# Splitting each weight once instead of once per batch, and one pool of seven buffers for it

## The chip, the core and the metric

The kernel runs on one core of a Trainium2 chip. The metric is device time in microseconds. The kernel before was timed three times: 928.41 us is the median, 927.8 the lowest and 928.49 the highest. The profile comes from one further execution, whose own span, from its first to its last instruction, is 930.6 us.

The core has these engines: PE (TensorE, the matrix multiplier; PEld is its loading of the stationary operand), DVE (VectorE), ACT (ScalarE), POOL (GpSimd) and SP (SyncE). Here SP only issues DMAs, in the order of its queue: a DMA whose buffer is not yet free holds up the DMAs behind it.

## The reference

Softcapped attention for 4 batches, 12 heads, 448 tokens and a head size of 64, then a gated feed-forward block over all 4 x 448 tokens.

```python
scores = cap * np.tanh(scale * (q @ k^T) / cap)
attn = exp(scores - max) / (sum(...) + 1e-09)
x = (attn @ v), heads side by side      # 1792 x 768
gate = 1 / (1 + np.exp(-(x @ w_gate)))  # w_gate, w_val: 768 x 1536
out = (gate * (x @ w_val)) @ w_out      # w_out: 1536 x 768
```

The activations come as float32. The weights reach the kernel as float64.

## The kernel before

**The arithmetic.** TensorE multiplies float32 values as pairs: x = hi + lo, where hi is x rounded to a shorter format (float32r) and lo = x - hi. A product is hi*lo + hi*hi + lo*hi, three passes. So every operand has to be *split*: `o.hi` (line 148; "p" is POOL, line 151) writes the rounded part, and `o.lo` (line 157; "v" is DVE, line 159) writes the rest. All splits by these helpers stand in the profile under lines 151 and 159, and are told apart by the tile they write.

**The weights.** The three weight matrices are cut into 36 units of 128 x 768 values: per group of four columns blocks of w_gate, four units, then four of w_val (24 units in all), then 12 units of w_out. The feed-forward of a batch uses units 0 to 35 in this order, and each of the four batches does so again: 144 uses, numbered u = 0 to 143.

- `load_w64` (line 590) loads a unit as float64, 768 KB, into one of three buffers (`w`).
- `convert_w` (line 596) makes float32 of it from the bits: one ACT instruction (line 609) and three DVE instructions (lines 610 to 612), into one of four buffers (`wx`, tag `wraw`). The float32 unit is then stored to DRAM (`wd`, 384 KB).
- `load_w` (line 635) reads a float32 unit back from DRAM into one of the same four buffers (`wraw`). That is needed for the first 12 units, which are converted during batch 0's attention and not kept (`o.early`), and for all units of batches 1 to 3: 120 loads of 384 KB.
- `split_w` (line 641) splits a unit with POOL and DVE into one of three buffers (`wspl`), two units ahead of its use. It runs for all 144 uses.
- `next_w` (line 674) is called before a unit's matmuls. It converts up to four units ahead during batch 0, loads three ahead, and splits two ahead.

**The stages.** Batch 0's attention runs alone (with the conversion of the first 12 units beside it). Then the feed-forward of batch b runs beside the attention of batch b+1, and the feed-forward of batch 3 runs alone at the end. The feed-forward has two parts: `h` (line 690, 24 units of 18 matmuls with 448 columns) and `o` (line 761, 12 units; 18 matmuls of 384 columns each, 30 in the last batch, which also takes the left-over tokens of all batches).

**Attention of batches 1 to 3.** Per head: transposes (line 282), scores (line 307), tanh and exp on ACT (lines 310 and 442), the split of the exponentials (`ph` on ACT at line 153, `pl` and the last part of `ph` on DVE), the sum over keys in three POOL additions (`a`, lines 317 to 319), in batches 2 and 3 a fold on DVE (line 322), the split of the sum (`as`: POOL, then DVE), the matmul of the sums (`dn`, line 395) and the product with V (`pv`, lines 381 to 384).

**What sets the order.** A list scheduler orders the instructions of each engine at build time. It takes the program order and its own estimate of when buffers come free. During batch 0's attention the order of PE and ACT is the one in which the code is written. On the chip each engine then works through its own list in order: where an instruction waits, everything behind it on that engine waits too.

Of the kernel before, what the change touches and what calls it, by code (L numbers as in the profile page):

```python
# [23 lines left out]
# Up to here exp(score) needs no maximum: |score| <= |cap|, so that every exponential lies between  # L24
# exp(-32) and exp(32).
# [4 lines left out]
def tile_softcap_attention_then_gated_ffn(  # L30
# [11 lines left out]
    """Softcapped attention, then a gated feed-forward block, in float32.  # L42

    TensorE multiplies float32 operands as pairs of float32r values: x = hi + lo, where hi is x
    rounded to 12 significant bits and lo = x - hi is exact, so hi*hi + hi*lo + lo*hi carries the
    product to float32's accuracy at one pass each.

    The softmax has two forms, chosen by the value of cap: exponentials of the scores as they are
    where cap bounds them, and with the maximum subtracted for any other cap.
    """  # L50
# [9 lines left out]
    # The first pair of heads is on its way before cap chooses.  # L60
# [8 lines left out]
    # TensorE's clock rises with some microseconds of work.  # L69
# [4 lines left out]
    # The score is even in cap.  # L74
# [20 lines left out]
def _load(nc, t, src, n, twice):  # L95
    """Both heads of pair n; the chunk after the full ones holds the last tokens, on either half
    when twice."""
# [15 lines left out]
def _load_heads_inside(nc, t, src, n):  # L113
    """The same, with both heads of a token side by side, and the last tokens once."""
# [12 lines left out]
class _Ops:  # L127
    """What both attentions share."""

    def __init__(self, tc, ctx, c, q, k, v):  # L130
# [4 lines left out]
        self.FULL = self.S // P * P  # tokens in the chunks of 128  # L135
# [12 lines left out]
    def hi(self, eng, dst, src):  # L148
        """dst (float32r) = src rounded."""
        if eng == "p":  # L150
            self.nc.gpsimd.tensor_scalar(dst, src, 1.0, 1.0, ALU.mult, ALU.mult)  # L151
        elif eng == "a":
            self.nc.scalar.activation(dst, src, AF.Copy)  # L153
        else:
            self.nc.vector.tensor_copy(dst, src)
# [12 lines left out]
def _bounded_attention(o, x_done):  # L168
    """Scores with keys on partitions; yields the PE passes (of 448 columns) that it has emitted,
    and None after a batch.  # L170

    Of the reference's denominator, sum(exp(s - max)) + 1e-9, both terms are taken times exp(max):
    sum(exp(s)) + 1e-9 * exp(max). The sum stands in for exp(max), which it bounds: in float32 the
    guard leaves a sum that holds exp(max) as it is.
    """
# [5 lines left out]
    # The sums of GS heads stand on one row each, rows 0.. (repeated up to 32): head i's stationary  # L181
    # operand has ones in the columns of its rows. Their reciprocals, hi on rows 0.., lo on rows
    # 32.., go to the 64 rows of each head through spread.
# [17 lines left out]
    # The first batch has TensorE to itself: products of its first heads are plain float32.  # L201
# [8 lines left out]
    def spare(h):  # L210
        """VectorE converts weights during the first two batches."""
# [23 lines left out]
    def split_pair(n):  # L235
# [6 lines left out]
        if n < NP and direct_v(2 * n):  # L242
            # Beside each head's V a block of ones, for the sums.
# [17 lines left out]
    def emit_T(h, step=None):  # L261
        """k and q with tokens along the free dimension: both heads of a pair in float32, or
        [hi; lo] of one head and q's [lo; hi]."""
# [71 lines left out]
    def emit_P(h):  # L335
        """The exponentials, split. The last chunk's upper copy becomes its low part."""
# [10 lines left out]
    def emit_PV(h):  # L347
# [6 lines left out]
        if direct_v(h):  # L354
            # The sums stand on the partitions of the other head.
# [30 lines left out]
        # The rows of V_hi and of V_lo meet on the partitions that the head has in x.  # L386
# [72 lines left out]
def _general_attention(o, x_done):  # L459
    """Queries on partitions, with each row's maximum subtracted; products are plain float32."""  # L460
# [87 lines left out]
def _emit(tc, ctx, c, attention_of, q, k, v, w_gate, w_val, w_out, out):  # L548
# [10 lines left out]
    WRAW = 4  # L559
    AHEAD = 2  # L560
# [296 lines left out]
```

## Time and profile before

| | |
|---|---|
| time, median of 3 (lowest to highest) | 928.41 us (927.8 to 928.49) |
| span of the profiled execution | 930.6 us |
| PE busy | 825.7 us, 89% |
| DVE busy | 709.5 us, 76% |
| POOL busy | 526.4 us, 57% |
| ACT busy | 458.2 us, 49% |
| DMA | 119.77 MB, 129 GB/s over the span |

Rows of instruction groups read: line, engine, operation, tile written <- tiles read, shapes, number; then busy time in us and the mean of one in ns; then the idle time of the engine just before these instructions and what ended most of it. In a table by stretches of time each row gives the stretch, its length, and for each engine the busy time and the number of instructions in it, then the granted TensorE clock as a share of full speed, the mean busy share of the 16 DMA engines, and GB/s. Rows of waits read: who waited <- for whom: us in total, times, longest. Busy time on PE includes slower running at a lower granted clock.

### The profile page before, as it was taken

The page shows a single profiled execution, that of the slowest core. Times are in us where ns is not written, and L with a number is a line of the kernel's source. Part 1 is how long each engine was busy: PE and PEld are TensorE (multiplying, and loading weights), DVE is VectorE, ACT ScalarE, POOL GpSimd, SP SyncE. Part 2 cuts the span into 40 slices and gives each one's busy share as a digit, 9 for nine tenths or more (in the row PEclk, how much of TensorE's full clock was granted, in tenths as well). Part 3 has the DMA queues.
Part 4 walks back from the last instruction along what each step waited for, and adds up shares of the span by engine and source line. Part 5 has one row for each costly group of instructions (what it writes and reads, how often), then busy time and mean ns, then how long its engine had stood idle before and what let it go on. Part 6 is the DMA issues. An engine that isn't in the chain of part 4 may idle for free. (4 is left out here: it accounts for less than half of the span.)

```text
span 930.6 us, 10942 instructions
## 1 busy us (share of the span) xinstructions
PE 825.7 (89%) x3890; PEld 696.3 (75%) x3890; DVE 709.5 (76%) x664; ACT 458.2 (49%) x601; POOL 526.4 (57%) x468
## 2 busy tenths in 40 slices
PE   8998899787886768988998798999898999999994
PEld 4443487666775757877887687888787889999994
DVE  0586877999999999798968898799959985455220
ACT  4796685573375642846446661848365612101000
POOL 1233689668588875675739565677738643233110
PEclk6998999888997889999999999999999999999998
DMA  6497842363557445323332534223232464334211
GB/s 171 134 281 237 260 133 76 122 213 108 166 172 218 153 134 158 91 63 103 86 118 59 140 109 135 91 80 102 74 119 63 122 191 134 111 122 120 73 61 46
DMA packets 114408, 119.77 MB, mean 129 GB/s; under 512 B 53928, under 2 KB 91304, under 8 KB 114344
## 3 DMA queue, kind: packets, MB, share of 16 engines
q1 hardware_dynamic: 114344, 118.98, 42.1%
q8 instruction: 33, 0.54, 0.2%
q14 instruction: 31, 0.25, 0.1%
HBM read 96.14 MB, written 22.02 MB: 127 GB/s over the span
## 5 line engine op out<-in xcount | busy, mean ns | idle before, releaser
L690 PE MATMUL h<-xspl,wspl 128*128 128x448 f32 x1728 | 397.5, 376 | 16.4 <-DVE wspl L159 12.6
L690 PEld LDWEIGHTS h<-xspl,wspl 128*128 128x128 f32 x1728 | 330.2, 193 | 53.4 <-DVE wspl L159 15.9
L159 DVE TENSOR_TENSOR wspl<-wraw,wspl 128x768 fp32r<-128x768 f32 x120 | 153.3, 1284 | 92.5 <-POOL wspl L151 90.6
L151 POOL TENSOR_SCALAR wspl<-wraw 128x768 fp32r<-128x768 f32 x120 | 116.9, 977 | 152.4 <-PE h L690 62.2
L761 PE MATMUL o<-wspl,gspl 128*128 128x384 f32 x864 | 175.2, 353 | 19.0 <-DVE wspl L159 17.4
L761 PEld LDWEIGHTS o<-wspl,gspl 128*128 128x128 f32 x864 | 161.9, 200 | 24.5 <-DVE wspl L159 20.5
L310 ACT ACTIVATE t<-sc,scale 128x448 f32<-128x448 f32 x192 | 115.6, 633 | 104.2 <-PE sc L307 98.6
L307 PE MATMUL sc<-T 128*128 128x448 f32 (+1 forms) x240 | 102.3, 481 | 4.2 <-ACT t L310 3.5
L442 ACT ACTIVATE t<-t,capv 128x1792 f32<-128x1792 f32 (+2 forms) x60 | 88.2, 1490 | 0.8
L159 DVE TENSOR_TENSOR pl<-t,ph 128x1344 fp32r<-128x1344 f32 x36 | 78.0, 2167 | 6.5 <-ACT ph L153 6.3
L317 POOL TENSOR_TENSOR a<-t 128x448 f32<-128x448 f32 x36 | 57.0, 1584 | 42.4 <-ACT t L442 24.8
L719 ACT ACTIVATE gate<-h 128x448 f32<-128x448 f32 x48 | 25.4, 544 | 92.1 <-PE h L690 74.5
L307 PEld LDWEIGHTS sc<-T 128*128 128x128 f32 (+1 forms) x240 | 44.0, 190 | 30.3 <-ACT t L310 13.9
L319 POOL TENSOR_TENSOR a<-a,t 64x448 f32<-64x448 f32 x36 | 62.1, 1726 | 0.9
L153 ACT ACTIVATE ph<-t 128x1792 fp32r<-128x1792 f32 x36 | 61.2, 1700 | 0.5
L609 ACT ACTIVATE wx<-w 128x768 f32<-128x768 f32 x36 | 32.6, 907 | 57.5 <-DVE wspl L159 41.6
L610 DVE TENSOR_SCALAR wx<-wx 128x768 int32<-128x768 int32 x36 | 29.2, 810 | 41.4 <-ACT wx L609 41.1
L318 POOL TENSOR_TENSOR a<-a,t 128x448 f32<-128x448 f32 x36 | 58.5, 1624 | 1.8
L381 PE MATMUL pv<-pl,vs 128*128 128x448 f32 x108 | 42.1, 390 | 19.0 <-DVE pl L159 19.0
L151 POOL TENSOR_SCALAR gspl<-gate 128x448 fp32r<-128x448 f32 x48 | 44.7, 932 | 24.0 <-DVE gate L721 23.7
L307 PE MATMUL sc<-qs,T 128*128 128x448 f32 x144 | 53.0, 370 | 3.7 <-DVE qs L296 3.7
L159 DVE TENSOR_TENSOR ph<-t,ph 64x448 fp32r<-64x448 f32 x36 | 51.1, 1418 | 1.1
(89 smaller groups left out, 1142.3 us busy)
## 6 DMA issues: line engine op xcount, KB each, us to landing
wraw<-wd SPq DMA_DIRECT2D x120, 384.0 KB, 3.0
wd<-wx SPq DMA_DIRECT2D x36, 384.0 KB, 2.9
w<-in_moe_w_gate_dram SPq DMA_DIRECT2D x12, 768.0 KB, 6.4
w<-in_moe_w_val_dram SPq DMA_DIRECT2D x12, 768.0 KB, 5.6
w<-in_moe_w_out_dram SPq DMA_DIRECT2D x12, 768.0 KB, 5.4
out_dram<-pair SPq DMA_DIRECT2D x8, 576.0 KB, 3.6
vn<-in_v_dram SPq DMA_DIRECT2D x23, 192.0 KB, 2.8
qkn<-in_q_dram SPq DMA_DIRECT2D x18, 192.0 KB, 2.5
```

Source lines behind the costliest of these rows:

```text
L151: self.nc.gpsimd.tensor_scalar(dst, src, 1.0, 1.0, ALU.mult, ALU.mult)
L153: self.nc.scalar.activation(dst, src, AF.Copy)
L159: e.tensor_sub(dst, src, hi.bitcast(F32))
L307: nc.tensor.matmul(ps[:n], kT[:, m * P:m * P + n], r, start=(i == 0), stop=(i == len(rhs) - 1))
L310: nc.scalar.activation(t[:n, m, :], ps[:n], AF.Tanh, scale=c["scale"][:n])
L317: nc.gpsimd.tensor_add(a, t[:, 0, :], t[:, 1, :])
L318: nc.gpsimd.tensor_add(a, a, t[:, 2, :])
L319: nc.gpsimd.tensor_add(a[0:R], a[0:R], t[0:R, NF, :])
L381: nc.tensor.matmul(pv, s[:, j * NC + m, :], pl[:, m, :], start=(m == 0), stop=False)
L442: nc.scalar.activation(x, x, AF.Exp, scale=c["cap"][:x.shape[0]])
L690: nc.tensor.matmul(ps, a, r, start=(kk == 0 and i == 0), stop=(kk == KD - 1 and i == 2))
L761: nc.tensor.matmul(ps, a, r, start=(x + kk == 0 and i == 0), stop=(x + kk == KF - 1 and i == 2),)
```

## The change

A unit is now split once, right after its conversion, and *both parts* are stored to DRAM (`wd` becomes 768 KB). Batches 1 to 3, and batch 0 for its first 12 units, read both parts back with one DMA and use them as they are. The number of splits falls from 144 to 36, the 36 stores grow from 384 to 768 KB, and so do the 120 loads.

The buffers change with it. One set of seven buffers of 768 KB (tag `w`) holds both the float64 units and the split units; there were three of each before, and four buffers of 384 KB for float32 units, of which two are left. The total is the same. A unit is loaded as far ahead as seven buffers allow; in batch 0, up to its last units, three of them are reckoned for float64. Conversion runs three units ahead, not four (`LEAD`). The first 12 units are split during batch 0's attention. Comments and docstrings are taken out, which moves line numbers: `h` matmuls stand at line 702 in the changed kernel (690 before), `o` at 773 (761), the conversion at 610 to 613 (609 to 612), the store of a unit at 646 (617), its load at 658 (638), the float64 load at 594 (593).

```diff
-    WRAW = 4
+    WRAW = 2
     AHEAD = 2
+    WB = 7
@@ load_w64
-            t = wp.tile([P, UN], I64, tag="w64", bufs=W64, name=f"w64_{u}")
+            t = wp.tile([P, UN], I64, tag="w", bufs=WB, name=f"w64_{u}")
@@ convert_w
-        d = dram.tile([P, UN], F32, name=f"wd{u}")
-        w_dram.append(d)
-        nc.sync.dma_start(out=d, in_=x)
-        if u >= o.early:
-            w_raw[u] = x
+        w_raw[u] = x
+        if u < o.early:
+            split_w(u)
@@
-    def load_w(u):
-        if u < o.early or NU <= u < B * NU:
-            t = wp.tile([P, UN], F32, tag="wraw", bufs=WRAW, name=f"wraw{u}")
-            nc.sync.dma_start(out=t, in_=w_dram[u % NU])
-            w_raw[u] = t
+    def new_w(u):
+        return wp.tile([P, 2, UN], F32R, tag="w", bufs=WB, name=f"wspl{u}")
 
     def split_w(u):
-        if u < B * NU:
-            t = w_raw.pop(u)
-            s = wp.tile([P, 2, UN], F32R, tag="wspl", bufs=AHEAD + 1, name=f"wspl{u}")
-            o.hi("p", s[:, 0, :], t)
-            o.lo("v", s[:, 1, :], t, s[:, 0, :])
+        if u not in w_raw:
+            return
+        t, s = w_raw.pop(u), new_w(u)
+        o.hi("p", s[:, 0, :], t)
+        o.lo("v", s[:, 1, :], t, s[:, 0, :])
+        d = dram.tile([P, 2, UN], F32R, name=f"wd{u}")
+        w_dram.append(d)
+        nc.sync.dma_start(out=d.bitcast(F32), in_=s.bitcast(F32))
+        if u >= o.early:
             w_spl[u] = s
+    loaded = {"next": 0}
+    def load_to(n):
+        while loaded["next"] < min(n, B * NU):
+            u = loaded["next"]
+            loaded["next"] += 1
+            if u < o.early or NU <= u:
+                t = new_w(u)
+                nc.sync.dma_start(out=t.bitcast(F32), in_=w_dram[u % NU].bitcast(F32))
+                w_spl[u] = t
@@
-    LEAD = 4
+    LEAD = 3
@@ next_w
-        load_w(u + AHEAD + 1)
+        load_to(u + (WB - W64 if u < NU - W64 else WB))
         split_w(u + AHEAD)
@@ before the first feed-forward
     convert_to(o.early)
-    for u in range(AHEAD + 1):
-        load_w(u)
-    for u in range(AHEAD):
-        split_w(u)
+    load_to(WB - W64 - 1)
```

The scheduler makes a new order of it. Three places are shown; numbers in the tile names are the unit or the head.

DVE beside the `o` part of batch 1's feed-forward, at heads 32 and 33 (`pl`, `ph`: exponentials; `a`, `as`: sums; `qs`, `qks`: q and k). Before:

```order
L159 TENSOR_TENSOR pl32_3869<-t32_3771,ph32_3868 128x1344
L159 TENSOR_TENSOR ph32_3868<-t32_3771,ph32_3868 64x448
L296 CAST qs34_3894<-T34_3891 64x448
L159 TENSOR_TENSOR wspl63_4150<-wraw63_4116,wspl63_4150 128x768
L322 TENSOR_TENSOR a32_3873<-a32_3873 64x448
L159 TENSOR_TENSOR wspl64_4215<-wraw64_4148,wspl64_4215 128x768
L159 TENSOR_TENSOR as32_3878<-a32_3873,as32_3878 64x448
L389 TENSOR_TENSOR xraw2_2880<-pv32_3962,tmp32_3991 64x448
```

and with the change:

```order
L159 TENSOR_TENSOR pl32_3809<-t32_3717,ph32_3808 128x1344
L159 TENSOR_TENSOR ph32_3808<-t32_3717,ph32_3808 64x448
L733 TENSOR_TENSOR gate1_2_3626<-h1_1_11_3981,gate1_2_3626 128x448
L296 CAST qs34_3834<-T34_3831 64x448
L322 TENSOR_TENSOR a32_3813<-a32_3813 64x448
L159 TENSOR_TENSOR xspl2_4032<-xraw2_2874,xspl2_4032 128x448 x3
L159 TENSOR_TENSOR gspl1_2817<-gate1_2_3626,gspl1_2817 128x448
L159 TENSOR_TENSOR as32_3818<-a32_3813,as32_3818 64x448
```

No weight split (`wspl`) stands between the fold `a` and the split `as` any more.

DVE where batch 0's feed-forward begins (`rd`: the softmax divisors of the last two heads of batch 0; `wx`: conversion). Before:

```order
L159 TENSOR_TENSOR wspl0_849<-wraw0_843,wspl0_849 128x768
L369 SCALAR_TENSOR_TENSOR rd5_764<-rd5_764 128x448
L370 RECIPROCAL rd5_764<-rd5_764 128x448
L159 TENSOR_TENSOR wspl1_852<-wraw1_845,wspl1_852 128x768
L373 TENSOR_TENSOR xraw0_235<-pv10_759,rd5_764 64x448
L373 TENSOR_TENSOR xraw0_235<-pv11_818,rd5_764 64x448
L159 TENSOR_TENSOR wspl2_875<-wraw2_847,wspl2_875 128x768
```

and with the change:

```order
L612 SCALAR_TENSOR_TENSOR wx13_1439<-w64_13_694,wx13_1439 128x768
L369 SCALAR_TENSOR_TENSOR rd5_798<-rd5_798 128x448
L613 SCALAR_TENSOR_TENSOR wx13_1439<-w64_13_694,wx13_1439 128x768
L370 RECIPROCAL rd5_798<-rd5_798 128x448
L373 TENSOR_TENSOR xraw0_235<-pv10_793,rd5_798 64x448
L373 TENSOR_TENSOR xraw0_235<-pv11_852,rd5_798 64x448
L159 TENSOR_TENSOR pl12_865<-t12_817,ph12_864 128x1344
```

The splits of units 0 to 11 have moved from here into batch 0's attention, and unit 13 is converted here; before, that came later in the order.

SP's queue a third of the way into batch 0's feed-forward, with what each DMA waits for (`qkn`, `vn`: q, k and v of a later pair of heads; DMAHW is the queue's own bookkeeping). Before:

```order
L617 DMA wd13_1378<-wx13_1373 128x768 [waits DMAHW1_49,DVE_49]
L593 DMA w64_16_1380<-in_moe_w_gate_dram 128x6x128 [waits DMAHW2_49,Activation_49]
L102 DMA qkn10_1341<-in_q_dram 128x2x192 [waits DMAHW3_49,Pool_49]
L107 DMA qkn10_1341<-in_q_dram 64x2x64 [waits DMAHW4_49]
L107 DMA qkn10_1341<-in_q_dram 64x2x64 [waits DMAHW5_49]
```

and with the change:

```order
L646 DMA wd12_1374<-wspl12_1371 128x1536 [waits DMAHW0_49,DVE_49]
L594 DMA w64_16_1444<-in_moe_w_gate_dram 128x6x128 [waits DMAHW1_49,PE_49]
L102 DMA qkn10_1339<-in_q_dram 128x2x192 [waits DMAHW2_49,Pool_49]
L107 DMA qkn10_1339<-in_q_dram 64x2x64 [waits DMAHW3_49]
L107 DMA qkn10_1339<-in_q_dram 64x2x64 [waits DMAHW4_49]
```

The store now waits for the split of its unit and not for the conversion alone, and the float64 load behind it waits for PE to finish with a unit, where it waited for ACT to have read a float64 buffer.

## The prediction

> **What bounds the kernel now.** The first view is the busy time of each engine by stretches, cut where a batch's first `h` matmul (line 690) starts; batch 0's feed-forward is cut once more where its thirteenth unit starts. I call the stretches A to F.
>
> ```profile
> core 0: us, PE busy (x) PEld busy (x) DVE busy (x) ACT busy (x) POOL busy (x), PEclk, DMA share, GB/s
> 0.00:108.80 108.80, 101.67 (x282) 45.79 (x283) 64.96 (x70) 78.07 (x118) 35.66 (x58) 0.89 0.72 218
> 108.80:190.70 81.90, 70.12 (x340) 60.15 (x340) 71.10 (x54) 49.48 (x64) 69.00 (x55) 0.96 0.38 116
> 190.70:361.00 170.30, 134.31 (x617) 117.98 (x615) 166.23 (x146) 91.44 (x115) 126.21 (x88) 0.88 0.53 169
> 361.00:571.50 210.50, 187.54 (x950) 166.28 (x951) 182.03 (x168) 117.51 (x150) 135.66 (x116) 0.98 0.34 99
> 571.50:767.70 196.20, 181.75 (x914) 162.69 (x913) 167.24 (x161) 106.84 (x135) 122.32 (x106) 0.97 0.37 109
> 767.70:930.60 162.90, 150.35 (x793) 143.45 (x792) 58.00 (x70) 14.91 (x20) 37.54 (x49) 0.98 0.31 95
> ```
>
> The page's first part gives the shares of the whole span, which hide that the limit changes:
>
> ```profile
> PE 825.7 (89%) x3890; PEld 696.3 (75%) x3890; DVE 709.5 (76%) x664; ACT 458.2 (49%) x601; POOL 526.4 (57%) x468
> ```
>  In C (units 12 to 35 of batch 0, with all the conversions) DVE is busy 166.23 of 170.3 us, 98%: DVE sets the end there. In D and E PE is busy 89% and 93% and DVE 86% and 85%: PE sets the pace, and DVE's queue delays it. In F, batch 3 alone, PE is busy except for the tail after the last matmul. B is between: both at 86%.
>
> What ends PE's idle time comes from the waits of PE, for D and then for E:
>
> ```profile
> PE dn L395 <- DVE as L159: 14.0, 8, 3.1
> PE pv L381 <- DVE pl L159: 3.9, 3, 1.8
> PE h L690 <- DVE wspl L159: 2.5, 2, 1.4
> ...
> PE dn L395 <- DVE as L159: 8.6, 7, 2.5
> PE o L761 <- DVE wspl L159: 2.7, 2, 2.1
> PE h L690 <- DVE wspl L159: 2.6, 2, 1.4
> PE pv L381 <- DVE pl L159: 2.1, 2, 1.9
> ```
>
> Nearly all of D's 23.0 us of idle PE (210.50 - 187.54) and of E's 14.5 (196.20 - 181.75) end on DVE, and mostly not on the weights but on the sums (`as`): the end of a chain POOL, POOL, POOL, DVE, POOL, DVE with weight splits queued between its links. Last, the chain that ended last shows that PE waits for nothing in F:
>
> ```profile
> 767.78 87.84 PE h L690 x432
> 855.62 62.45 PE o L761 x360
> ```
>
> A unit there takes 87.84 / 24 = 3.66 us in `h` and 62.45 / 12 = 5.20 us in `o`.
>
> **The change part by part.** The instructions that go are these (DVE's groups in D, in E, in F, in B, then POOL's in D):
>
> ```profile
> L159 DVE TENSOR_TENSOR wspl<-wraw,wspl 128x768 fp32r<-128x768 f32 x37 | 50.5, 1373 | 9.4 <-POOL wspl L151 8.4
> ...
> L159 DVE TENSOR_TENSOR gspl<-gate,gspl 128x448 fp32r<-128x448 f32 x12 | 11.6, 968 | 1.4 <-POOL gspl L151 1.4
> ...
> L159 DVE TENSOR_TENSOR wspl<-wraw,wspl 128x768 fp32r<-128x768 f32 x37 | 47.5, 1288 | 11.7 <-POOL wspl L151 10.8
> ...
> L159 DVE TENSOR_TENSOR wspl<-wraw,wspl 128x768 fp32r<-128x768 f32 x34 | 37.5, 1106 | 64.7 <-POOL wspl L151 64.7
> ...
> L159 DVE TENSOR_TENSOR gspl<-gate,gspl 128x448 fp32r<-128x448 f32 x12 | 7.4, 613 | 0.5 <-POOL gspl L151 0.5
> ...
> L159 DVE TENSOR_TENSOR wspl<-wraw,wspl 128x768 fp32r<-128x768 f32 x12 | 16.9, 1419 | 6.6 <-POOL wspl L151 6.6
> ...
> L151 POOL TENSOR_SCALAR wspl<-wraw 128x768 fp32r<-128x768 f32 x37 | 40.0, 1083 | 22.1 <-PE h L690 13.8 <-DVE wspl L159 4.7 <-issue 2.5
> ```
>
> *Stretch D: -21 us.* 50.5 us of DVE and 40.0 us of POOL work disappear; DVE falls to 131.5 us, 69% of a stretch of 190. The waits for `wspl` go directly, those for `as` because the weight splits no longer stand inside that chain. What stays is the chain itself and the exponentials, so I don't take all. As an estimate, the delay behind a queue goes with share / (1 - share): 0.86 / 0.14 = 6.1 now, 0.69 / 0.31 = 2.2 then, about a third, so 23.0 us become 8; with the waits for `wspl` gone wholly I leave 6. That takes 17 us of idle time. PE's busy time is 5.8 us longer than E's for the same work; I take 4 of it, as slower pace around idle moments. Bounds: nothing, and 28.8 us (all idle time, and E's busy time).
>
> *Stretch E: -11 us.* The same: 47.5 us leave DVE, 65% of 185 us is left, and 0.85 / 0.15 = 5.7 becomes 1.9. Of 14.5 us of idle time a third stays and 10 go, and 1 of busy time. Bounds 0 and 14.5.
>
> *Stretch B: -9 us.* The 12 splits move to A: 16.9 of 71.10 us of DVE work. PE idles 11.8 us; I take three quarters. Bounds 0 and 11.8.
>
> *Stretch C: +2 us.* Here little goes: the splits of units 12 to 35 stay, and so do the conversions (the three DVE instructions of each), so DVE stays at its limit. The change takes two of the four float32 buffers away. ACT, which begins a conversion, already waits for a buffer (the waits of ACT in C, then those over the whole span):
>
> ```profile
> ACT wx L609 <- DVE wspl L159: 25.3, 4, 10.0
> ACT wx L609 <- DMA w<-in_moe_w_out_dram: 10.3, 3, 5.8
> ...
> ACT wx L609 <- DVE wspl L159: 41.6, 6, 11.2
> ```
>
> While ACT waits there, the tanh and exp of the next head wait behind it, and then PE. With two buffers it waits more often; DVE's other work covers that as long as DVE is at 98%. I take +2. If the cover fails and half of the 25.3 us again reaches DVE it is +12; a better order could give -5. SP's queue gets the two new waits (a store for its split, a float64 load for PE); behind them stand the loads of q, k and v for a later pair of heads and the next units, which are needed several units later.
>
> *Stretch A: +1 us.* Twelve splits of 1.4 us on DVE (17 us on 64.96 of 108.8) and of 1.1 us on POOL (13 on 35.66) lie beside PE. The end would feel them only if each of the six softmax divisions waited behind one split: 6 x 1.4 = 8 us, the upper bound. The twelve stores grow by 4.7 MB on 218 GB/s x 108.8 us = 23.7 MB, so the DMA share goes from 0.72 to about 0.86, which stays below 1. The first unit's load now stands in the queue behind the store of unit 11; PE has the scores of heads 12 and 13 meanwhile.
>
> *Stretch F: 0.* DVE and POOL get emptier, and PE waits for neither now. What is new is the load: 786,432 B per 3.66 us is 215 GB/s, where now it is half. For that, these rows:
>
> ```profile
> wraw<-wd SPq DMA_DIRECT2D x120, 384.0 KB, 3.0
> w<-in_moe_w_gate_dram SPq DMA_DIRECT2D x12, 768.0 KB, 6.4
> grest<-gspl SPq DMA_DIRECT2D x3, 768.0 KB, 5.9
> GB/s 171 134 281 237 260 133 76 122 213 108 166 172 218 153 134 158 91 63 103 86 118 59 140 109 135 91 80 102 74 119 63 122 191 134 111 122 120 73 61 46
> ```
>
> The third slice moved 281 GB/s in this kernel, with short rows from the float64 weights and q, k, v. A load of 768 KB should land in about 6 us (5.9 and 6.4 above); with seven buffers six are under way or waiting while one is used, which is 6 x 3.66 = 22 us ahead. So it is covered. Bounds 0 and, as a rival, +62.
>
> *Sum.* +1 - 9 + 2 - 21 - 11 + 0 = -38; 930.6 - 38 = 892.6 for the profiled execution. That one is 2.2 us above the median of the timed runs (928.41), so **890 us**.
>
> **The rivals.**
>
> *1. All the idle time goes (868 us).* B, D and E give their bounds and C 5: 11.8 + 28.8 + 14.5 + 5 = 60 instead of 38. For it: DVE's other instructions are slowed by POOL's, as `gspl` shows: 968 ns in D beside POOL at 64%, 613 ns in F at 23%. With 40 us of POOL work gone, the links of the chain get shorter too. Against it: the POOL additions of the sums stay, and C has the same POOL work. [...]
>
> *2. The waits only move (917 us).* The chain of the sums is long by itself; if the scheduler has placed the `dn` matmuls by its own estimate, PE stands at them anyway. Then half of B, D and E comes (4.5 + 8 + 5), and C loses 5 more than nothing, A 1: 930.6 - 17.5 + 6 = 919, less 2.2. For it: the `as` waits are at most 3.1 us each, many and small. Against: each link now waits for a DVE at 69%.
>
> *3. The loads become the bound (952 us, slower).* If in F the loads follow one another instead of overlapping, a unit takes 5.9 us instead of 3.66 and 5.20: 24 x 2.24 + 12 x 0.7 = 62 us on top of 890. In D and E a unit takes 210.5 / 36 = 5.8 us, so nothing is lost there. It decides once less than 5.9 / 3.66 = 1.6 loads overlap. For it: one queue carries all, with the stores of left-over tokens and outputs between. Against: 281 GB/s in the third slice. [...]
>
> That the splits stay is excluded: the new order holds one pair of split instructions per unit, 36.
>
> **How the numbers follow.** Forecast 0.57, with its own range 878 to 902 (each of the terms for D, B and C off by half at once); rival 1 0.17; rival 2 0.19; rival 3 0.07. Within 0.2% of 928.4 means within 1.9 us, about what a measurement can tell. Faster: the first two and nearly all of rival 2, 0.91; the same 0.02, from the slow end of rival 2; slower 0.07. The range takes in the forecast, about half of rival 1 down to 866 and of rival 2 up to 916, and leaves out rival 3.
>
> **What would show it.** Right: PE's idle time in D and E at about 6 and 5 us, `dn` waits below half, DVE there near 70%; C still about 170 us with DVE near 98%; F unchanged with 30 loads of 768 KB and no PE wait for a DMA. Rival 1 would show in `gspl` at about 620 ns in D; rival 2 in `dn` waits as long as before; rival 3 in PE waiting on `wspl<-wd` loads in F. The prediction fails if C grows by over 12 us through ACT waiting at the conversion, or if F grows at all.

## The result and the profile after

The changed kernel takes **897.78 us** (median of 4 runs, 894.8 to 898.06). The kernel before took 928.45 us beside it (927.8 to 929.05). The ratio is 0.967, with a 95% interval from 0.963 to 0.972: faster by 31 us. The forecast was 890 us, 38 us faster. One execution of e7 below (1010.39 us) and one of the kernel before (2663.12 us, beside e12) ran in a far slower state and enter no ratio, but e7's median is given over all four of its executions (892.94 us without the slow one).

The profiled execution of the changed kernel has a span of 895.7 us. First its engines over the whole span, from the page's first part; then the view by stretches (busy us and instructions of each engine, then granted clock, DMA share and GB/s), cut at the same places as A to F of the kernel before.

```profile
PE 822.2 (92%) x3890; PEld 696.8 (78%) x3890; DVE 545.8 (61%) x556; ACT 462.0 (52%) x601; POOL 397.9 (44%) x360
```

```profile
core 0: us, PE busy (x) PEld busy (x) DVE busy (x) ACT busy (x) POOL busy (x), PEclk, DMA share, GB/s
0.00:124.70 124.70, 111.23 (x300) 51.43 (x301) 90.63 (x93) 87.55 (x130) 58.14 (x76) 0.85 0.82 262
124.70:186.00 61.30, 61.30 (x312) 54.44 (x310) 33.06 (x30) 39.18 (x49) 41.84 (x35) 1.00 0.49 157
186.00:374.40 188.40, 146.71 (x663) 127.73 (x661) 176.83 (x157) 103.23 (x132) 129.58 (x92) 0.86 0.65 217
374.40:554.30 179.90, 176.89 (x917) 161.23 (x917) 115.38 (x125) 109.25 (x138) 83.18 (x76) 0.99 0.61 202
554.30:731.40 177.10, 174.25 (x912) 158.70 (x912) 110.08 (x122) 107.88 (x135) 78.33 (x72) 1.00 0.59 195
731.40:895.70 164.30, 151.81 (x793) 143.31 (x791) 19.81 (x33) 14.90 (x20) 6.81 (x12) 0.97 0.49 165
```

| stretch | before | after | change | forecast |
|---|---|---|---|---|
| A, attention of batch 0 | 108.8 | 124.7 | +15.9 | +1 |
| B, units 0 to 11 | 81.9 | 61.3 | -20.6 | -9 |
| C, units 12 to 35 of batch 0 | 170.3 | 188.4 | +18.1 | +2 |
| D, batch 1 | 210.5 | 179.9 | -30.6 | -21 |
| E, batch 2 | 196.2 | 177.1 | -19.1 | -11 |
| F, batch 3 | 162.9 | 164.3 | +1.4 | 0 |

The counts of matmuls in parentheses are a warning for this table: the new order puts some of the work on the other side of a cut. A has 18 matmuls more than before (300, not 282), B 28 fewer (312, not 340), C 46 more (663, not 617), D 33 fewer (917, not 950). At E's mean of 181.75 us / 914 = 0.2 us each, D gave about 6.6 us of its work to A to C. A to D together hold the same work in every kernel here (about 2190 matmuls), so I compare A to D as one number: 571.5 us before, 554.3 after, **-17.2** where the forecast's terms add up to -27. E is the cleanest stretch, with 911 to 916 matmuls everywhere.

What PE waits for in D and then in E, whole lists:

```profile
PE dn L395 <- DVE as L159: 2.9, 2, 1.9
...
PE dn L395 <- DVE as L159: 2.9, 2, 1.8
```

The waits for `wspl` and `pl` are gone, and of the 14.0 and 8.6 us for `as` 2.9 are left each. In F PE waits for nothing, as before. In C PE idles longer than before (41.7 us, not 36.0), and ACT stands at the conversion more often: these are PE's largest waits in C, then ACT's there.

```profile
PE pv L381 <- DVE pl L159: 12.6, 4, 7.1
PE o L773 <- DVE wspl L159: 9.0, 5, 3.2
PE dn L395 <- POOL as L151: 8.6, 3, 7.0
...
ACT wx L610 <- DVE wspl L159: 39.5, 15, 7.5
```

ACT waited there 4 times for 25.3 us; now it is 15 times for 39.5 us.

Most of DVE's other instructions got shorter too. Three of DVE's groups in D and E together, the kernel before first, then the two that remain in the changed one:

```profile
L159 DVE TENSOR_TENSOR wspl<-wraw,wspl 128x768 fp32r<-128x768 f32 x73 | 97.0, 1336 | 21.0 <-POOL wspl L151 19.1
L159 DVE TENSOR_TENSOR as<-a,as 64x448 fp32r<-64x448 f32 x24 | 17.6, 733 | 1.0
L389 DVE TENSOR_TENSOR xraw<-pv,tmp 64x448 f32<-64x448 f32 x24 | 14.9, 621 | 3.3 <-ACT tmp L388 2.7
```

```profile
L159 DVE TENSOR_TENSOR as<-a,as 64x448 fp32r<-64x448 f32 x23 | 14.2, 619 | 5.4 <-POOL as L151 4.9
L389 DVE TENSOR_TENSOR xraw<-pv,tmp 64x448 f32<-64x448 f32 x23 | 14.3, 621 | 45.6 <-ACT tmp L388 45.4
```

`as`, with both inputs in SBUF, fell from 733 to 619 ns. `xraw`, with one input in PSUM, stayed at 621. Not every group got shorter: `pl` went from 1784 to 1974 ns. DVE's busy time in D and E fell from 349.3 to 225.5 us, which is 26.8 us more than the 97.0 of the splits; some 7 of it, as an estimate from the numbers of instructions and their means, is the one head that moved to C. The first split row shows something that I had not counted: 21.0 us in which DVE stood idle at the head of its queue, 19.1 of them because POOL's half of the split was not ready.

### The profile page after: what moved, and what is told of

Same layout as the page of the kernel before. It is cut to its first block, busy times and chain, and to the rows that moved or that the text cites. A ratio compares the mean times of both kernels' runs of the same rounds, so it can differ in the third digit from the quotient of the medians.

```text
span 895.7 us, 10552 instructions
## 1 busy us (share of the span) xinstructions
PE 822.2 (92%) x3890; PEld 696.8 (78%) x3890; DVE 545.8 (61%) x556; ACT 462.0 (52%) x601; POOL 397.9 (44%) x360
## 2 busy tenths in 40 slices
DMA packets 114405, 181.09 MB, mean 202 GB/s; under 512 B 53928, under 2 KB 91304, under 8 KB 114344
## 4 chain that ended last, share of the span: by engine, by line
PE 60%; DVE 21%; issue 6%; ACT 5%; POOL 4%; DMA 1%; SPq 1%; DVEq 0%; POOLq 0%
PE h L702 27%; PE o L773 17%; PE sc L307 7%; PE pv L359 3%; DVE wspl L159 3%; DVE wx L612 2%; DVE pl L159 2%; DVE wx L613 2%; PE tp L282 2%; DVE ph L159 2%; DVE qs L296 2%; DVE wx L611 2%; PE pv L381 1%; PE pv L382 1%; ACT t L310 1%
## 5 line engine op out<-in xcount | busy, mean ns | idle before, releaser
L702 PEld LDWEIGHTS h<-xspl,wspl 128*128 128x128 f32 x1728 | 325.8, 190 | 34.6 <-issue 0.9
L773 PE MATMUL o<-wspl,gspl 128*128 128x384 f32 x864 | 171.8, 352 | 14.2 <-DVE wspl L159 9.0
L773 PEld LDWEIGHTS o<-wspl,gspl 128*128 128x128 f32 x864 | 161.1, 200 | 18.7 <-DVE wspl L159 11.2
L151 POOL TENSOR_SCALAR gspl<-gate 128x448 fp32r<-128x448 f32 x48 | 37.8, 787 | 141.9 <-DVE gate L733 140.8
L317 POOL TENSOR_TENSOR a<-t 128x448 f32<-128x448 f32 x36 | 50.5, 1403 | 91.5 <-ACT t L442 85.2
L159 DVE TENSOR_TENSOR pl<-t,ph 128x1344 fp32r<-128x1344 f32 x36 | 71.5, 1986 | 26.7 <-ACT ph L153 26.3
L733 DVE TENSOR_TENSOR gate<-h,gate 128x448 f32<-128x448 f32 x48 | 29.8, 620 | 85.7 <-PE h L702 85.3
L151 POOL TENSOR_SCALAR wspl<-wx 128x768 fp32r<-128x768 f32 x36 | 40.3, 1121 | 78.9 <-DVE wx L613 53.1
L288 ACT ACTIVATE T<-tp 128x512 fp32r<-128x512 f32 (+1 forms) x84 | 46.1, 563 | 26.4 <-PE tp L282 25.9
L389 DVE TENSOR_TENSOR xraw<-pv,tmp 64x448 f32<-64x448 f32 x36 | 22.3, 620 | 59.4 <-ACT tmp L388 59.0
L159 DVE TENSOR_TENSOR gspl<-gate,gspl 128x448 fp32r<-128x448 f32 x48 | 45.2, 942 | 16.5 <-POOL gspl L151 16.0
```

Of the source, the lines that this page charges most:

```text
L159: e.tensor_sub(dst, src, hi.bitcast(F32))
L288: nc.scalar.activation(t[:, base:base + width], ps.bitcast(F32), AF.Copy)
L317: nc.gpsimd.tensor_add(a, t[:, 0, :], t[:, 1, :])
L702: nc.tensor.matmul(ps, a, r, start=(kk == 0 and i == 0), stop=(kk == KD - 1 and i == 2))
L773: nc.tensor.matmul(ps, a, r, start=(x + kk == 0 and i == 0), stop=(x + kk == KF - 1 and i == 2),)
```

## The experiments

No kernel here leaves out any of the reference's work; where work is added, it is said. Times are medians; the ratio is to the kernel before, run beside them. Beside the experiments the kernel before took 921.6 to 935.6 us, so a difference of a few us between two versions is near the noise; the stretches come from one profile of each kernel. The theory at the start: in D and E the gain is DVE's (and POOL's) lighter queue; in A to C the shared buffers and the early splits took part of it back. The rivals: the larger stores and loads cost the time in A to C; in D and E it was TensorE's wait for a split, or the deeper loads, that went.

### Batch 0 as before, both parts kept (e1)

Batch 0 gets its former buffers (three for float64, three for split units, four for float32), its lead of four units, and the float32 copies of the first 12 units. Each split unit is stored all the same (768 KB), and batches 1 to 3 read it into the same six large buffers, alternately.

```diff
...
+            elif NU <= u:
+                tag, bufs = ("wspl", AHEAD + 1) if u % 2 else ("w64", W64)
+                t = wp.tile([P, 2, UN], F32R, tag=tag, bufs=bufs, name=f"wspl{u}")
+                nc.sync.dma_start(out=t.bitcast(F32), in_=ws_dram[u % NU].bitcast(F32))
...
```

> Batch 0 as before (three float64 buffers, four float32, three split; the first 12 units kept as float32 and split at their use), but each split unit is also stored; batches 1 to 3 read both parts back, alternately into the float64 and the split buffers (six). Changed kernel: stretches A to C (up to batch 1's feed-forward) 374.4 us, D 179.9, E 177.1, F 164.3. If the new order of buffers and the early splits cost the 13.4 us by which A to C grew (361.0 before), A to C is back at 361 to 365 here, D to F stay as in the changed kernel, and the time is about 880 to 886. If the larger stores themselves cost it, A to C stays at 370 to 376 and the time at about 897.

Measured: 888.18 us, ratio 0.956 (0.950 to 0.963), 2 us above the first theory's range. A to D 544.4 us, 9.9 less than the changed kernel; D 182.4 and E 178.6 stay as after. It moves as many bytes (181.10 and 181.09 MB). So the larger stores and loads as such cost nothing that can be seen, and about 10 us of A to D were the price of batch 0's new buffers and order.

### Six shared and four float32 buffers (e2)

```diff
-    WRAW = 2
+    WRAW = 4
-    WB = 7
+    WB = 6
```

> The changed kernel with six shared buffers and four float32 buffers (the same memory). If A to C grew because ACT's conversions wait for one of two float32 buffers (41 us of such waits, 17 times), those waits fall below 25 us, A to C shrinks to about 360 to 366 and the time to about 885. If it is the shared buffers, or the DMAs at the end of A, or the early splits, A to C stays at 374 or grows, and the time is 897 or more.

Measured: 891.69 us, ratio 0.960 (0.951 to 0.969). A to D 548.0 us, 6.3 less than the changed kernel; the time lies between the two theories. ACT waits at the conversion in C as before the change:

```profile
ACT wx L610 <- DVE wspl L159: 26.7, 4, 9.0
```

So two float32 buffers instead of four cost about 6 us, with the waits that the prediction named. These 6 us are near the noise here; the same edit is tried once more below (e10). A stays long at 120.8 us, so it has another cause.

### Eight early units instead of twelve (e7)

```diff
-    o.early = 12
+    o.early = 8
```

> The changed kernel with 8 units stored and read back in batch 0 instead of 12. The end of A has its transfers at a DMA share of 0.98 to 0.99. If these cost A its 16 us, A falls by a third of that and more, to 112 to 116, and C, with VectorE at 94% and four more conversions and splits in it, grows by 4 x 5 = 20 us less what B's idle VectorE takes: the total 896 to 904, no gain. If A's growth is VectorE's work instead (the early splits), A falls by the same 4 x 1.4 = 6 us, to 119, and the total is 898 to 906.

Measured: 893.28 us, ratio 0.959 (0.952 to 0.965), below both ranges. A falls from 124.7 to 109.3 us, more than either theory said and far more than four DVE splits, but four conversions leave A with them; A to D falls by 5.8 to 548.5. These are 30 us at the end of A in the changed kernel:

```profile
95.00:125.00 30.00, 22.05 (x67) 12.01 (x64) 28.62 (x24) 20.17 (x30) 21.92 (x16) 0.77 1.01 353
```

The DMA engines are full (share 1.01) at 353 GB/s: stores of split units, the first loads of them, float64 loads and the next heads' q and k come together. That is not enough to call them the cause. Here are 20 us around the end of this version's A (at 109.3 us), then 10 us of e1, after the end of its A:

```profile
100.00:110.00 10.00, 9.61 (x31) 5.57 (x32) 9.84 (x9) 6.51 (x11) 9.26 (x7) 0.83 1.00 348
110.00:120.00 10.00, 6.17 (x28) 5.48 (x27) 9.84 (x10) 7.40 (x9) 7.25 (x4) 0.87 1.03 362
```

```profile
110.00:120.00 10.00, 10.00 (x46) 8.97 (x47) 7.37 (x7) 5.87 (x9) 6.58 (x7) 0.83 1.04 332
```

The DMA engines are as full there, and in e1 PE is busy all the time beside it. PE's longest wait at the end of the changed kernel's A is this one:

```profile
120.15 1.13 PE L282 MATMUL tp<-ident_r,qks 128*128 128x128 f32 x7 [4.80 <-POOL qks L159]
```

It is for POOL's split of q and k (`qks`). POOL came to that split without waiting for a load: just before it had split v, for which it had waited 2.0 us for PE, and earlier 3.7 us for DVE's `xraw`, while DVE, with conversions and early splits in its queue, was busy for 28.62 of the 30 us. e2, with twelve early units too, has nearly as much idle PE in A, 13.1 us, at a mean DMA share of 0.78; the changed kernel has 13.5 us at 0.82. With eight early units the wait for `qks` is gone. This speaks for the early units' work on POOL and DVE; but ACT waits once for a load in these 30 us, for 4.4 us, so the transfers may have a part. No run takes one away and leaves the other, so the cause of A's growth stays open.

The 353 GB/s are a mean over these 30 us and no ceiling: of the 0.75 us slices in them the fastest, 1.5 us in, moved 452 GB/s.

### Both together (e10)

```diff
-    o.early = 12
+    o.early = 8
-    WRAW = 2
+    WRAW = 4
-    WB = 7
+    WB = 6
```

> The version with six shared buffers and four float32 buffers (891.7 us; A 120.8, B 73.2, C 167.5), with 8 early units instead of 12. If the transfers at the end of A and the missing float32 buffers in C are two separate costs: A falls to about 110, C grows by the four conversions less what four buffers cover, about 8 us, total 884 to 890. If VectorE's work in C decides, C grows by 4 x 4.6 = 18 us and the total is 893 to 901.

Measured: **882.71 us**, ratio 0.950 (0.945 to 0.955), the fastest version here, below even the first theory's range. Its stretches A to C, D, E and F:

```profile
0.00:353.50 353.50, 301.37 (x1243) 219.72 (x1244) 299.13 (x270) 219.64 (x295) 233.14 (x197) 0.92 0.69 224
353.50:538.90 185.40, 181.94 (x947) 164.99 (x946) 125.58 (x134) 117.88 (x151) 87.22 (x81) 0.99 0.60 196
538.90:717.60 178.70, 175.80 (x912) 160.26 (x912) 110.16 (x122) 107.95 (x135) 78.44 (x72) 0.99 0.60 193
717.60:882.20 164.60, 151.82 (x793) 143.32 (x791) 19.82 (x33) 14.91 (x20) 6.82 (x12) 0.97 0.51 171
```

A to D is 538.9 us, 15.4 less than the changed kernel. The two edits alone gave 6.3 and 5.8: two separate costs, with some 3 us more when both go. The buffers now give about 10 us in the time (893.28 to 882.71), so their cost is seen twice. ACT's waits for a float32 buffer over A to C, in this kernel and then in the changed one:

```profile
ACT wx L610 <- DVE wspl L159: 6.1, 2, 3.6
```

```profile
ACT wx L610 <- DVE wspl L159: 44.7, 20, 7.5
```

### Sixteen and ten early units in e1's version (e8, e11)

Each changes only `o.early` of e1's kernel.

> The version that was fastest so far (batch 0 as in the kernel before, both parts stored beside it, read back in batches 1 to 3; 888.2 us), with 16 early units instead of 12. Four conversions move from C, where VectorE is at its limit, to A, where it is busy for less than two thirds. If VectorE's work alone sets C: C falls by 4 x 3.2 = 13 us, A grows by less than 4, total 877 to 882. If the transfers at A's end set A (four more stores and 8 more 64-bit loads of 768 KB, at 330 GB/s 2.4 us each): A grows by 10 and more, and the total is 886 to 892.

Measured: 895.17 us, ratio 0.961 (0.956 to 0.966), above both ranges. A grew by 21.6 to 127.4 us, and A to D from 544.4 to 553.6, although less conversion is left in C. PE waits for `t` in A, and ACT, which makes it, stands at conversions for float64 loads:

```profile
ACT wx L609 <- DMA w<-in_moe_w_gate_dram: 5.7, 3, 4.1
ACT wx L609 <- DMA w<-in_moe_w_val_dram: 5.5, 1, 5.5
```

So more early units do not pay here either. ACT's waits for loads are 11.2 us of the 21.6; on the mean the DMA engines are no fuller in A than in e1 (share 0.72, in e1 0.74).

> The version with batch 0 as in the kernel before (888.2 us; A 105.8, B 81.9, C 174.3; 12 early units), with 10 early units. Its A has TensorE busy but for 6 us, so there is little to win in A; C, at VectorE's limit, gets two more conversions, of which B's idle VectorE takes some: 888 to 894. Below 886 would mean that even this A is held by its transfers.

Measured: 894.62 us (887.95 to 896.79), ratio 0.964 (0.959 to 0.969), just above the expected range; no gain over e1. Its profile is that of its shortest run, so its stretches (A to D 542.9 us) say little on the median.

### One engine's splits put back, with nobody waiting (e3, e4)

Each unit read back gets an instruction whose result nobody reads: in e3 a VectorE subtraction, in e4 a GpSimd multiplication, of the split's size.

```diff
+                if u >= NU:
+                    z = wp.tile([P, UN], F32, tag="wraw", bufs=WRAW, name=f"z{u}")
+                    nc.vector.tensor_sub(z, t[:, 0, :].bitcast(F32), t[:, 1, :].bitcast(F32))
```

In e4 the last line is `nc.gpsimd.tensor_scalar(z, t[:, 0, :].bitcast(F32), 1.0, 1.0, ALU.mult, ALU.mult)`.

> The changed kernel, with one DVE subtraction of 128 x 768 added for each unit read back in batches 1 to 3, into a buffer that nobody reads: DVE's part of the removed splits is back, POOL's is not, and nothing waits for it on the way to PE. If D and E gained because DVE's queue got shorter, most of the 49.7 us comes back: D about 200 and E about 188 us, the time 920 or more. If they gained because POOL and DVE hold each other off less, about a third comes back: 910. If the units simply wait less for their own split, nothing: 898.

> The same with one POOL multiplication of 128 x 768 for each unit instead, so that POOL's part is back and DVE's is not. If DVE's queue is the cause, D and E stay near 180 and 177 us, and the time is 898 to 902. If POOL and DVE holding each other off is the cause, DVE's other instructions get longer again (gspl in D toward 968 ns from what it is now), D and E grow by 10 us or more each, and the time is about 918.

Measured: 906.33 us (ratio 0.976, 0.967 to 0.985) and 911.91 us (0.982, 0.973 to 0.991). E of e3, then E of e4:

```profile
558.10:742.60 184.50, 177.93 (x915) 160.54 (x915) 146.81 (x160) 106.98 (x135) 79.03 (x70) 0.99 0.58 184
```

```profile
561.20:746.10 184.90, 178.15 (x912) 161.31 (x911) 120.79 (x121) 107.60 (x135) 115.64 (x108) 0.98 0.58 187
```

Neither alone brings the loss back: E grows by 7.4 and 7.8 us of 19.1, D by 2.9 and 3.8. My expectation for DVE's queue alone was missed. The e4 row shows the other thing: DVE's busy time in E rises from 110.08 to 120.79 us with the same instructions, while GpSimd's goes from 78.33 to 115.64. The instructions show it too; this is `as` in D and E of e4:

```profile
L159 DVE TENSOR_TENSOR as<-a,as 64x448 fp32r<-64x448 f32 x23 | 21.2, 923 | 8.3 <-POOL as L151 7.9
```

It went from 619 to 923 ns, and `gspl` from 789 to 993; `xraw`, with an input in PSUM, stayed at 621. So these instructions of VectorE did get longer with more GpSimd work beside them, at a smaller price (911.91 us) than the 918 that I gave.

### Both put back, off the line and on it (e6, e5, e12)

e6 has both idle instructions per unit. e5 splits each unit read back once more in place, two units ahead, with the values unchanged, so that TensorE waits for it as before the change:

```diff
+        if NU <= u < B * NU:
+            t = w_spl[u]
+            hi, lo = (t[:, i, :].bitcast(F32) for i in range(2))
+            nc.gpsimd.tensor_scalar(t[:, 0, :], hi, 1.0, 1.0, ALU.mult, ALU.mult)
+            nc.vector.scalar_tensor_tensor(t[:, 1, :], hi, 0.0, lo, ALU.mult, ALU.add)
```

> The changed kernel with both idle instructions per unit read back in batches 1 to 3: one GpSimd multiplication and one VectorE subtraction, 128x768 each, written to the two float32 buffers that nobody reads, and TensorE waits for neither. The amount of work of the kernel before on both engines, but off the line to TensorE. If the loss is in the amount of work (both engines hold each other off): D near 203, E near 195, total 930 to 940, as much as the version that splits again. If the loss lies in TensorE waiting for a split: the two losses of the single runs added, D near 187, E near 192, total 915 to 922.

> The changed kernel, where in batches 1 to 3 each unit read back (both parts, 768 KB, into the seven buffers as changed) is split once more in place before TensorE uses it, two units ahead as in the kernel before: GpSimd multiplies the high part by one, then VectorE makes the low part from it. TensorE waits for both, so the splits are back in the line, with nothing else of the change undone. Theory 1 (the gain in D and E is the two engines' work and the splits' place in their queues): D near 208 and E near 194, together 402 of the 406.7 us before, and the total 938 to 948, slower than before since A to C stays at 374. Theory 2 (idle dummies showed some 10 us each, and the rest came from the buffers: loads now come seven units ahead, and a unit waits for none): D near 188, E near 186, total 912 to 918.

Measured: e6 942.77 us (1.013, 1.006 to 1.020), e5 931.12 us (1.003, 0.999 to 1.006). D and E of e6, then of e5, and PE's only waits above 1 us in D and E of e5:

```profile
374.60:575.30 200.70, 184.04 (x914) 165.53 (x913) 168.66 (x157) 109.28 (x138) 134.27 (x113) 0.95 0.55 180
575.30:777.40 202.10, 184.52 (x915) 163.52 (x914) 161.88 (x160) 107.02 (x135) 123.89 (x105) 0.97 0.53 172
```

```profile
371.40:568.00 196.60, 182.19 (x913) 165.24 (x912) 172.72 (x157) 107.92 (x136) 128.47 (x111) 0.96 0.57 183
568.00:763.90 195.90, 180.57 (x911) 161.89 (x911) 164.32 (x158) 106.87 (x135) 120.81 (x105) 0.97 0.54 175
```

```profile
PE dn L395 <- DVE as L159: 27.5, 13, 5.2
```

With the work back, E is 195.9 us on the line and 202.1 off it; before the change it was 196.2. Off the line it costs as much or more, and on the line PE waits for the sums (`as`) and never for `wspl`. So TensorE's wait for a split, the rival in D and E, is refuted as the main part: the gain is the two engines' work, felt through the chain of the sums. Deeper loading, the other rival, is out for E: e5 has it as well, and the loss is back whole. In D it is not back whole: e5 loses 16.7 us there (179.9 to 196.6, at about the same number of matmuls) of the 24 that the change gained like for like, and the time, 931.12 us, lies between the two theories. For the remaining 7 or so the rivals stay open.

One doubt about e6: its idle instructions stand at the head of a queue until a load has landed (60.5 us on GpSimd, 35.6 us on VectorE in D and E), and what is behind them waits. e12 issued them where TensorE takes the unit, seven units later.

```diff
         split_w(u + AHEAD)
+        if u >= NU:
+            hi, lo = (w_spl[u][:, i, :].bitcast(F32) for i in range(2))
...
         return w_spl.pop(u)
```

> As the version with both idle instructions per unit read back (D 200.7, E 202.1), but each issued where TensorE takes the unit, some seven units after its load was begun, so that neither GpSimd nor VectorE stands in its queue waiting for a load (there 60 us of GpSimd's and 36 us of VectorE's time in D and E together). The amount of work is the same. If the work itself costs the time (TensorE waits for none of it, the other work on both engines gets later): D and E together stay above 390, total 926 to 942. If it was the waiting for loads at the head of the queues: D and E together 360 to 375, total 900 to 916.

Measured: 941.91 us (1.012, 1.008 to 1.015), as e6. But these two rows of e12, for D and E, show the same waits for loads:

```profile
L694 POOL TENSOR_SCALAR z<-wspl 128x768 f32<-128x768 f32 x73 | 88.5, 1212 | 65.4 <-DMA wspl<-wd 63.2 <-issue 1.6
L696 DVE TENSOR_TENSOR zz<-wspl 128x768 f32<-128x768 f32 x73 | 87.0, 1192 | 38.1 <-DMA wspl<-wd 36.7
```

The instructions stand close behind the loads again, so e12 repeats e6 and does not decide the doubt.

### More VectorE work alone (e9)

e3 with a second idle subtraction of 128x512 per unit, meant to give VectorE as much as with both engines' work, and GpSimd nothing.

```diff
...
+                    z = wp.tile([P, UN], F32, tag="wraw", bufs=WRAW, name=f"zz{u}")
+                    nc.vector.tensor_sub(z[:, 0:512], hi[:, 0:512], lo[:, 0:512])
```

> The changed kernel with two idle VectorE subtractions per unit read back in batches 1 to 3, 128x768 and 128x512, TensorE waits for neither, and GpSimd has none. VectorE's busy time rises to about 165 us in each of D and E, what it has with both idle instructions, but GpSimd keeps its 80 us. If VectorE's amount alone decides: D and E near 198 each, total 927 to 935. If it takes both engines (the links of the sums' chain on GpSimd get longer too, and the two engines hold each other off): D and E near 188, total 908 to 916.

Measured: 936.37 us, ratio 1.009 (1.005 to 1.013). D and E:

```profile
375.60:571.60 196.00, 181.37 (x908) 163.15 (x909) 178.40 (x192) 107.23 (x134) 96.67 (x73) 0.97 0.56 183
571.60:773.00 201.40, 183.49 (x916) 163.60 (x915) 180.74 (x198) 107.62 (x136) 90.21 (x70) 0.97 0.54 171
```

More work on VectorE alone costs as much as both engines' work, but it is more than I meant to give: 178.40 and 180.74 us of busy time, where e6 has 168.66 and 161.88; and GpSimd's busy time in E rises with it, from 78.33 to 90.21 us with the same instructions. VectorE's idle instructions in D and E, in e3 and then here:

```profile
L662 DVE TENSOR_TENSOR z<-wspl 128x768 f32<-128x768 f32 x73 | 77.9, 1069 | 40.5 <-DMA wspl<-wd 39.6
```

```profile
L663 DVE TENSOR_TENSOR z<-wspl 128x768 f32<-128x768 f32 x73 | 79.0, 1083 | 18.8 <-DMA wspl<-wd 17.5
L665 DVE TENSOR_TENSOR zz<-wspl 128x512 f32<-128x512 f32 x73 | 68.3, 936 | 0.0
```

VectorE waited for loads for 17.5 us here and for 39.6 in e3, so it lost more while it waited less for loads: that speaks for the amount of work, and against the doubt above as the main part. E by VectorE's busy time:

| | DVE busy | GpSimd busy | PE idle | clock | E |
|---|---|---|---|---|---|
| after | 110.1 | 78.3 | 2.9 | 1.00 | 177.1 |
| e4 | 120.8 | 115.6 | 6.8 | 0.98 | 184.9 |
| e3 | 146.8 | 79.0 | 6.6 | 0.99 | 184.5 |
| e6 | 161.9 | 123.9 | 17.6 | 0.97 | 202.1 |
| e5 | 164.3 | 120.8 | 15.3 | 0.97 | 195.9 |
| before | 167.2 | 122.3 | 14.5 | 0.97 | 196.2 |
| e9 | 180.7 | 90.2 | 17.9 | 0.97 | 201.4 |

Up to 147 us (80% of the stretch) VectorE's own work costs 7 us; the next 15 to 35 us cost another 11 to 18. VectorE's busy time does not order all rows: e4 loses 7.8 us at 120.8, and e6 as much at 161.9 as e9 at 180.7. So GpSimd's work counts as well: its idle instructions bring 7.8 us alone (e4), and beside VectorE's they lift its busy time from 146.8 to 161.9. How much of e6 is GpSimd's own lateness in the chain and how much the longer VectorE instructions stays open.

## Why the prediction was right, and where not

**The mechanism held in the main.** The gain is in D, E and B, it comes with the `as` waits, and putting both engines' work back takes E's gain away. But I sized the terms by DVE's share alone, and DVE's work alone (e3) gives back only 2.9 of D's and 7.4 of E's gain: it takes the work of both engines, or more of DVE's than went (e9).

**The sum came out near by luck.** The result lies 8 us above the forecast, within its own range, and the ratio says faster, as forecast. By stretches the terms missed by +15 (A), +16 (C) and +1.4 (F), and by -12 (B), -10 (D) and -8 (E): errors of 62 us that cancel to 3. Part of those in A to D is matmuls on the other side of a cut; over A to D together I forecast 10 us too much gain, over E 8 too little. Most of the other 5 us is my base: I took off 2.2 us to come from the profiled span to a time, but a time is longer than the span of its own execution (897.52 us for 895.7), so I estimate that the profiled execution before lay about 4 us above the median, not 2.2.

**The range and rival 2 were reckoned wrongly.** D, B and C off by half at once are 10.5 + 4.5 + 1 = 16 us, not the 12 of the range. Half of D is 10.5, not 8, so rival 2 comes to about 914 us.

**D, -21: nearly right.** PE's idle time fell from 23.0 to 3.0 us (forecast 6 left). Of the 30.6 us, 6.6 are the 33 matmuls that moved to A to C, which I had not read off the order; 24 are like for like. The 4 us of busy time had a wrong reason: I called D's and E's work the same, but the rows that I read say 950 and 914 matmuls, and at 0.2 us each that is 7 us, more than the whole difference of 5.8.

**E, -11 with -14.5 as its bound: too small, and the bound was wrong.** The idle time fell by 11.6 us (forecast 10). PE's busy time fell by 7.5, where I took 1 and took E's busy time as a floor. It is no floor. These are three windows of 4 us in E before, the first two neighbours, and then, from the timeline, the matmul at the end of PE's gap in the first of them:

```profile
615.50:619.50 4.00, 2.15 (x11) 1.54 (x11) 3.64 (x6) 1.50 (x3) 3.07 (x3) 0.99 0.52 173
619.50:623.50 4.00, 4.00 (x14) 3.62 (x13) 3.51 (x2) 0.81 (x2) 4.00 (x4) 0.58 0.14 27
...
759.50:763.50 4.00, 4.00 (x24) 4.00 (x24) 3.97 (x3) 0.58 (x1) 0.84 (x1) 1.00 1.00 262
```

```profile
617.54 0.39 PE L395 MATMUL dn<-as,pick 128*32 128x448 f32 x1 [1.85 <-DVE as L159]
```

After a wait of 1.85 us the granted clock was 0.58 in the next 4 us, with 14 matmuls instead of 24. That is 10 matmuls late, or, as an estimate, 10 x 4 / 24 = 1.7 us on top of the 1.85. E before has three such windows (at 571.5, 619.5 and 755.5 us, granted clock 0.57, 0.58 and 0.57), by the same estimate about 5 of the 7.5 us, each behind a wait of PE (2.48, 1.85 and 2.07 us); in E after the granted clock is 1.00. Not every such wait is followed by one. Another of 1.85 us ended at 719.71 us, and the window there is this:

```profile
719.50:723.50 4.00, 3.61 (x21) 3.05 (x21) 3.79 (x6) 2.07 (x2) 0.56 (x1) 1.00 0.76 167
```

So of two waits of 1.85 us one went before a window at 0.58 and one before a window at 1.00. What tells them apart was not shown.

**B, -9:** PE no longer waits there at all (61.30 of 61.3 us busy), more than the three quarters that I took; 28 matmuls, about 6 us of its 20.6, are on the other side of a cut.

**A, +1: the step that failed.** I bounded A by DVE's splits at the softmax divisions and set the transfers aside at a mean DMA share of 0.86. A grew by 15.9 us. PE idles 6.3 us more in it, all at POOL's split of q and k, a wait that the prediction does not have; the rest is busy time, 18 matmuls and a lower granted clock (0.85, before 0.89). The transfers were mis-sized too: A moved 32.7 MB where I reckoned 23.7 + 4.7, in part because I left out the first loads of split units (five of 768 KB by the end of A, where there were three of 384). e7 shows the price of four of the twelve early units in A to D as 5.8 us, and 15.4 in A itself. Whether it was the early work on DVE and POOL or the transfers stays open.

**C, +2, up to +12: mis-sized.** The mechanism was named (ACT at the conversion, two float32 buffers), and the 6.3 us by which e2 shortens A to D lie inside the bound. C itself grew by 18.1, beyond the 12 at which I said the prediction fails; 46 matmuls that came in from elsewhere are about 9 of it. The statement that DVE's other work covers ACT's waits did not hold: DVE is at 94% instead of 98%.

**F, 0: nearly.** No wait of PE, and the loads land in 4.4 us (the median of all 120). But F grew by 1.4 us, and I had said that the prediction fails if F grows at all, so by its own sign it fails here. Rival 3, for which that sign stood, is not the reason: its wait for a load is absent. The 1.4 us are taken up below.

**The rivals.** Rival 1 has the better half of D and E: its cause, VectorE's instructions slowed by GpSimd's, shows in `as` (733 to 619 ns, 923 in e4). Its own sign came half way: `gspl` in D fell from 968 to 765 ns, not to 620; over D and E it went from 952 to 789, and to 993 in e4. Its total failed at A and C. Rival 2 is refuted by the `as` waits, 22.6 us to 5.8. Rival 3 is refuted by F.

## What to carry to other kernels

Here work of an engine that TensorE didn't wait for directly still cost time, and not in proportion: from the changed kernel to e3, 37 us of VectorE's work in E cost 7 us; from e3 to e9, 34 more cost 17. When early work is to be moved into a quieter stretch, look at the end of that stretch in windows of some 10 us, for the engines as well as the transfers: a mean over the stretch hides where they meet (the DMA share was 0.82 over A of the changed kernel, 1.01 in its last 30 us). Full DMA engines there are a place to look, not yet a cause: see what the engine that PE waits for was itself waiting for. And when buffers are merged, look at what the small ones did: here two float32 buffers of 384 KB were worth more than the seventh large one (6.3 us of A to D in e2, about 10 us in the time from e7 to e10).

## What the runs showed of the hardware that I had not expected

**After a wait of 1.85 us on TensorE the granted clock was 0.58, one time of two.** It was so over the next 4 us, which with the wait cost about 3.5 us by the estimate above; behind another wait of 1.85 us it stayed at 1.00. Every D and E here with less than 8 us of idle PE has a clock of 0.98 to 1.00, and every one with over 13 has 0.94 to 0.98.

**A busy VectorE goes with a slightly faster F.** The `h` matmuls in F of before, after, e3 and e4, with no waits of PE in any and a granted clock of 1.00:

```profile
L690 PE MATMUL h<-xspl,wspl 128*128 128x448 f32 x432 | 87.9, 366 | 0.0
```

```profile
L702 PE MATMUL h<-xspl,wspl 128*128 128x448 f32 x432 | 89.4, 368 | 0.0
```

```profile
L705 PE MATMUL h<-xspl,wspl 128*128 128x448 f32 x432 | 87.8, 365 | 0.0
```

```profile
L705 PE MATMUL h<-xspl,wspl 128*128 128x448 f32 x432 | 89.4, 368 | 0.0
```

F is 1.4 us longer after the change. The loads are not the cause, since e3 and e9 move the same bytes and have 87.8 us. With VectorE work for each unit (before, e3, e9) it is 87.8 to 87.9, with GpSimd's alone (e4) 89.4. I have no explanation, and no run was made for it.
